# A one-layer decode kernel: five trips of the loop over head groups instead of four, and w_down split 11 rows per partition plus 128 rows on partitions 0 to 31

## The chip, the cores and the metric

The kernel runs on one core of a Trainium2 chip. The metric is device time of the whole program in microseconds (us); the kernel before has a median of 292.48 us over three runs (292.47 to 292.49). Engines are named as in the profile: PE is the matrix engine TensorE (PEld its weight loads), DVE VectorE, ACT ScalarE, POOL GpSimd, SP the engine that issues nearly all DMA transfers. A DMA transfer is cut into packets that up to 16 DMA engines move side by side.

## What is computed

One decode step of a transformer layer for two sequences, in bfloat16, with D = 640, 32 heads of 192, a window of the last 2048 cached positions, and a gated FFN of width F = 1536:

```python
x = A_x                                             # 2 x 1 x 640
q = layernorm(x) @ wq                               # 32 heads of 192
k, v = k_cache[..., -2048:, :], v_cache[..., -2048:, :]
h = x + softmax(q k^T / sqrt(192)) v @ wo
out = h + (gelu(layernorm(h) @ w_gate) * (layernorm(h) @ w_up)) @ w_down
```

Each weight and each cached key and value is used once, so the work is mostly reading: 122.29 MB come from HBM.

## The kernel before, in words

The program is written out as a list of operations with the tokens that each reads and writes (`_Prog`, from L50). From these it works out which semaphore each operation waits for. The operations of PE and DVE inside the loop get their wait values as a straight line in the trip number, so that one copy of the code serves all trips. This asks that every semaphore grows by the same amount in each trip; operations that do not run in every trip are counted on semaphores of their own (the class, `cls`, of an operation; the segments listed in `RARE`).

**The stream of loads.** SP issues all large loads in one order through one queue into a ring of 6 slots of 24,576 bytes per partition (`RING`, `pump`, L363). A load is issued as soon as what lay in its place has been used, so an SP instruction that waits holds back all loads behind it. The order is k(0), wq, k(1), then for g = 0 to 15 k(g+1) and v(g), with the output weights wo(0) behind v(3), wo(1) behind v(7), wo(2) and wo(3) behind v(15), and then w_gate, w_up and w_down. Each k or v tile is 3 MiB: one batch row, four heads, 2048 positions, with 64 positions of one head in the 24,576 bytes of each partition. w_down (1536 rows of 640) lies with 6 consecutive rows on each partition, twice, and comes in four transfers of 6, 3, 2 and 1 rows for each partition (`WDC`).

**The attention.** There are 16 tiles g, four to a group J of eight heads. For each g, PE turns the keys round (48 transposes at L574, copied out of PSUM by DVE at L588 and by ACT at L584), multiplies with the masked queries (`scores`, L635), DVE and ACT make the softmax (`softmax`, L644 to L655), PE brings the exponentials into columns (`e_columns`, L664), and `pv` (L680) adds up the values. `e_columns` and `pv` of tile g-1 are done between the steps of tile g. At the end of a group, `z_rows` (L694), `o_rows` (L705) and `o_columns` (L713) normalize and turn round the result, and `oproj(J)` (L731) multiplies with wo(J), one group later.

Tile 0, q and their masks stand ahead of the loop. The loop has four trips of tiles 4J+1 to 4J+4; in its fourth trip the last quarter is skipped. Behind the loop stand the end of tile 15, `o_rows(3)`, `oproj(2)`, `o_columns(3)` and `oproj(3)`.

**The end.** After `oproj(3)` comes the second layernorm, then for w_gate and w_up four matmuls for each of the five 128-row pieces c of D (`ffn_in`, L822; four column strips of 384 at once). `ffn_columns` (L831) turns the two results into columns with three transposes each; DVE and ACT make the gelu and the product `uT` (12 columns for each sequence). The w_down multiplication (L871) has 48 matmuls, four at a time, one transfer after the other; DVE copies the result (L877) and SP stores it (L878).

## Time and profile before

| what | value |
|---|---|
| median of the runs | 292.48 us (292.47 to 292.49) |
| the profiled execution's own time | 292.58 us |
| its span, first to last instruction | 291.3 us |
| around the span | 1.28 us |
| PE, DVE, ACT, POOL busy | 198.6, 122.8, 76.9, 25.7 us |
| mean granted clock of PE | 0.871 |
| bytes moved | 122.44 MB in 6506 packets, 420 GB/s over the span |

The profile is of one execution, which took 0.10 us longer than the median. Busy shares are of the span; the lines of the profile numbered L are those of the kernel before. A transfer lands when the last of its DMA engines has reported; the trace keeps one landing event for each engine that took part, and the start and length of each packet, but not which engine moved it.

### The profile page before, as it was taken

Reading aid. Unit: us, or ns where it says so; the run is one execution under the profiler, and the core shown is the slowest. Engines: PE = TensorE matmul, PEld = TensorE weight load, DVE = VectorE, ACT = ScalarE, POOL = GpSimd, SP = SyncE. Lnnn points to the kernel's source line nnn. Section 1 sums busy time; section 2 is a strip of 40 time slices with the busy share of each in tenths; the row PEclk is TensorE's granted clock in tenths of the full one; section 3 lists DMA queues with packets and bytes.
Section 4 is the critical chain, followed back from the end, with each engine's and each line's share of the span. In section 5 each row is a group of like instructions: output and inputs, shape, how many; then the busy total and the mean of one; then the engine's idle time right before and its main releaser. Section 6 shows DMA issues by size and latency. Waiting matters only on the chain.

```text
span 291.3 us, 5093 instructions
## 1 busy us (share of the span) xinstructions
PE 198.6 (68%) x2141; PEld 147.6 (51%) x2141; DVE 122.8 (42%) x231; ACT 76.9 (26%) x72; POOL 25.7 (9%) x85
## 2 busy tenths in 40 slices
PE   0650868786668288768677478868478778496684
PEld 0640437566355175637374475645465746472341
DVE  4350025455435334635356244635247445253331
ACT  1050014333322122423222123523142333151001
POOL 8820073000000000000000000000000000000000
PEclk9997568999979869997989579999689799688957
DMA  8999999999999999999999999999999999999994
GB/s 324 432 440 422 428 432 432 428 429 429 428 419 440 432 432 432 429 432 432 432 416 448 432 432 430 432 412 429 432 432 425 422 432 432 429 432 434 420 411 181
DMA packets 6506, 122.44 MB, mean 420 GB/s; under 512 B 734, under 2 KB 864, under 8 KB 1504
## 3 DMA queue, kind: packets, MB, share of 16 engines
q1 hardware_dynamic: 6348, 121.90, 97.8%
q10 hardware_dynamic: 148, 0.40, 0.4%
q8 instruction: 7, 0.11, 0.2%
q14 instruction: 3, 0.02, 0.0%
HBM read 122.29 MB, written 0.00 MB: 420 GB/s over the span
## 4 chain that ended last, share of the span: by engine, by line
DMA 73%; PE 18%; DVE 3%; issue 2%; SPq 2%; ACT 1%; DVEq 0%
DMA ring<-in_A_k_cache_dram 54%; PE tpp L574 13%; DMA ring<-in_A_wq_dram 10%; DMA ring<-in_B_w_down_dram 9%; DVE ktr L588 3%; PE tpp L598 2%; SPq L363 2%; PE ops L680 1%; DVE ering L428 1%; ACT ktr L584 1%; PE m L731 1%; PE m L713 1%; PE m L871 0%; PE m L694 0%; DVE yrow L877 0%
## 5 line engine op out<-in xcount | busy, mean ns | idle before, releaser
L574 PE MATMUL tpp<-identf,ring 128*128 128x128 f32 x768 | 116.2, 314 | 39.3 <-DMA ring<-in_A_k_cache_dram 25.2
L574 PEld LDWEIGHTS tpp<-identf,ring 128*128 128x128 f32 x768 | 102.8, 163 | 47.5 <-DMA ring<-in_A_k_cache_dram 26.5
L588 DVE COPY ktr<-tpp 128x2048 bf16<-128x2048 bf16 x64 | 78.4, 1224 | 91.4 <-PE tpp L574 91.4
L584 ACT ACTIVATE ktr<-tpp 128x2048 bf16<-128x2048 bf16 x32 | 60.1, 1877 | 94.9 <-PE tpp L574 94.9
L655 ACT ACTIVATE eexp<-sm,nm 128x512 bf16<-128x512 f32 x16 | 11.6, 722 | 71.7 <-DVE nm L653 71.7
L635 PE MATMUL sps<-ktr,rq 128*16 128x512 bf16 x384 | 25.7, 402 | 1.1 <-POOL rq L428 1.1
L680 PE MATMUL ops<-ring,ering 128*32 128x384 bf16 x512 | 25.0, 339 | 0.0
L644 DVE CUSTOM_DVE_ANT_1 sm<-sps,mska 128x512 f32<-128x512 f32 x16 | 11.0, 686 | 27.0 <-issue 27.0
L428 POOL TENSOR_TENSOR rq<-qs,mask 128x96 bf16<-128x96 bf16 x16 | 5.5, 354 | 175.6 <-PE sps L635 154.1
L680 PEld LDWEIGHTS ops<-ring,ering 128*32 128x32 bf16 x512 | 12.7, 99 | 8.5 <-issue 2.8
L635 PEld LDWEIGHTS sps<-ktr,rq 128*16 128x16 bf16 x384 | 8.9, 89 | 14.4 <-issue 5.5
L651 PEld LDWEIGHTS m<-mrhs,pm 128*128 128x128 bf16 x16 | 1.5, 96 | 22.9 <-DVE mrhs L424 22.9
L651 PE MATMUL m<-mrhs,pm 128*128 128x16 bf16 x16 | 2.9, 184 | 14.8 <-DVE mrhs L424 14.8
L598 PE MATMUL tpp<-ring,xnT 128*32 128x384 bf16 x80 | 6.1, 499 | 9.4 <-DMA ring<-in_A_wq_dram 9.4
L598 PEld LDWEIGHTS tpp<-ring,xnT 128*32 128x32 bf16 x80 | 3.4, 143 | 11.9 <-issue 9.6
L621 DVE CAST qs<-ops 128x384 bf16<-128x384 f32 x1 | 0.6, 558 | 15.8 <-PE ops L616 15.8
L428 DVE TENSOR_TENSOR ering<-m,mask 128x256 bf16<-128x256 f32 x16 | 6.6, 415 | 1.3 <-PE m L664 1.3
L713 PE MATMUL m<-selb,orow 128*128 128x2 bf16 x48 | 3.5, 200 | 5.2 <-DVE ering L428 4.5
L713 PEld LDWEIGHTS m<-selb,orow 128*128 128x128 bf16 x48 | 3.2, 159 | 6.0 <-DVE ering L428 4.9
L664 PE MATMUL m<-sel,eexp 128*128 128x64 bf16 x64 | 4.8, 200 | 1.2 <-ACT eexp L655 1.2
L494 PE MATMUL m<-identb,xrow 2*128 2x2 bf16 x5 | 0.3, 173 | 7.4 <-DMA xrow<-in_A_x_dram 7.4
L428 DVE TENSOR_TENSOR orow<-m,wm 128x1536 bf16<-128x1536 f32 x3 | 5.3, 1751 | 0.0
(127 smaller groups left out, 93.6 us busy)
## 6 DMA issues: line engine op xcount, KB each, us to landing
ring<-in_A_k_cache_dram SPq DMA_DIRECT2D x16, 3072.0 KB, 29.5
ring<-in_A_v_cache_dram SPq DMA_DIRECT2D x16, 3072.0 KB, 25.4
ring<-in_A_wq_dram SPq DMA_DIRECT2D x1, 7680.0 KB, 28.1
ring<-in_A_wo_dram SPq DMA_DIRECT2D x4, 1920.0 KB, 21.6
ring<-in_B_w_gate_dram SPq DMA_DIRECT2D x1, 1536.0 KB, 31.4
ring<-in_B_w_up_dram SPq DMA_DIRECT2D x1, 1536.0 KB, 21.9
ring<-in_B_w_down_dram SPq DMA_DIRECT2D x1, 960.0 KB, 24.3
ring<-in_B_w_down_dram SPq DMA_DIRECT2D x1, 480.0 KB, 25.0
```

Source lines behind the costliest of these rows:

```text
L363: P.op("sp", lambda e, v=v, src=src: e.dma_start(v, src), W=toks + [("sem", sem)], dma=sem)
L428: return lambda e: e.tensor_tensor(out=out, in0=a, in1=b, op=op)
L574: ins = e.transpose(tpp[bi][:, 512 * j + 128 * u:512 * j + 128 * (u + 1)], kv[:, off:off + 128], identf[:, :])
L584: act(lambda e, dst=dst, bv=bv: e.activation(out=dst, in_=bv, func=ACT.Copy), W=[("kt", half, k)], X=both)
L588: dve(lambda e, dst=dst, bv=bv: e.tensor_copy(dst, bv.rearrange("p (a x) -> p a x", a=2)), W=[("kt", half, k)], X=both, cls=0)
L598: ins = e.matmul(tps[0][32 * r:32 * (r + 1), 0:384], lhsT=xnT[:, c, 32 * J:32 * (J + 1)], rhs=wq[:, c, 1536 * J + 384 * r:1536 * J + 384 * ...
L635: ins = e.matmul(sps[32 * ch:32 * ch + 16, :], lhsT=rq[:, g % 4, k, :], rhs=ktr[:, k // 2, 1024 * ch + k % 2:1024 * (ch + 1):2], start=(k ...
L644: dve(lambda e: e.tensor_tensor_reduce(out=sm[:, :].rearrange("p (u x) -> p u x", u=4), in0=sps[:, :].rearrange("p (u x) -> p u x", u=4), ...
L655: act(lambda e: e.activation(out=eexp[:, :], in_=sm[:, :], func=ACT.Exp, bias=nm[:, 0:1], scale=1.0, accum_out=zr[:, g % 4:g % 4 + 1]), R= ...
L664: ins = e.matmul(o, lhsT=eexp[:, 128 * u:128 * (u + 1)], rhs=sel64[:, :], start=True, stop=True)
L680: ins = e.matmul(ops_[32 * r:32 * (r + 1), 0:384], lhsT=ering[:, g % 4, t, :], rhs=vv[:, 384 * t:384 * (t + 1)], start=(g % 4 == 0 and t < 4),
L713: ins = e.matmul(m2[:, 2 * kk:2 * kk + 2], lhsT=orow[:, :, kk:DH:12], rhs=selb[:, :], start=True, stop=True)
```

## The change

**The loop.** There are now five trips, and nothing of the attention but `oproj(3)` is left outside. A trip J begins with the transposes of tile 4J (not in the fifth). Then come, in trip 0 alone, `q_rows` and `q_stationary`; in the later trips the end of tile 4J-1 (`e_columns`, `z_rows`, `pv`, `o_rows`), from the third trip on `oproj(J-2)`, and `o_columns(J-1)`. Then, but for the fifth trip, scores and softmax of tile 4J, and the tiles 4J+1 to 4J+3. To keep the straight line of the waits, some semaphores start from an offset (`BIAS`, `WO_BIAS`), and there are three more of them. The program of PE has 744 matmuls in place of 858.

**Loads.** wo(0) is loaded behind v(7) in place of v(3), wo(1) behind v(11) in place of v(7), wo(2) behind v(15) as before, now into the slot of k(15). `oproj(2)` adds into `hrow` like the first two, and the residual x is added by two small matmuls in `oproj(3)` instead. w_up goes to the slot of k(14).

**w_down.** Rows 0 to 1407 lie with 11 consecutive rows on each partition, in transfers of 5, 3, 2 and 1 rows. The last 128 rows lie on partitions 0 to 31 alone, four rows each, in a transfer of their own (`wds`) ahead of the other four. Strip 3 of the gate and up results then is made of two matmuls, of 256 and 128 columns, so `ffn_in` has 5 matmuls for each c; `ffn_columns` has 9 transposes in place of 3; `uT` has 16 columns for each sequence, and w_down takes 60 matmuls in place of 48.

```diff
-WDC = ((0, 6), (6, 9), (9, 11), (11, 12))
+WDC = ((0, 5), (5, 8), (8, 10), (10, 11))
+NS = 11
-WO_AT = (K_AT[3], K_AT[3], K_AT[2], 0)
+WO_AT = (K_AT[3], K_AT[3], K_AT[3], 0)
+WU_AT = K_AT[2]
+WDS_AT = K_AT[1] + 12288
...
-            wd = B_w_down.rearrange("(q p s) n -> q p s n", p=128, s=6)
+            load("wds", WDS_AT, 8 * D, B_w_down[128 * NS:F, :].rearrange("(c a u) n -> a c (u n)", a=8, u=4), lambda v: v[0:32, :], "wds")
+            wd = B_w_down[0:128 * NS, :].rearrange("(p s) n -> p s n", s=NS)
...
-            if g % 4 == 3 and g < NG - 5:
-                load_wo(g // 4)
-        load_wo(2)
+            if g % 4 == 3 and g > 3:
+                load_wo(g // 4 - 1)
         load_wo(3)
...
-                    if J == 2:
+                    if J == 3:
                         for h in range(2):
                             e.matmul(m1[32 * h:32 * h + 2, 192:512], lhsT=identb[0:2, 0:2], rhs=xrow[0:2, 320 * h:320 * (h + 1)],
...
+        looped.append(True)
+        for J in range(5):
+            if J < 4:
+                P.loop_seg("d0", J)
+                transposes(4 * J, 0)
+                transposes(4 * J, 1)
+            if J == 0:
+                P.loop_seg("q", J)
+                q_rows()
+                q_stationary()
+            else:
+                P.loop_seg("y0", J)
+                e_columns(4 * J - 1)
+                z_rows(J - 1)
+                pv(4 * J - 1)
+                o_rows(J - 1)
+            if J > 1:
+                P.loop_seg("op", J)
+                oproj(J - 2)
+            if J > 0:
+                P.loop_seg("oc", J)
+                o_columns(J - 1)
+            if J < 4:
+                P.loop_seg("a0", J)
+                scores(4 * J)
+                softmax(4 * J)
+                for g in range(4 * J + 1, 4 * J + 4):
+                    transposes(g, 0)
+                    e_columns(g - 1)
+                    transposes(g, 1)
+                    pv(g - 1)
+                    scores(g)
+                    softmax(g)
         P.loop_seg()
-        e_columns(15)
...
-        oproj(2)
-        o_columns(3)
         oproj(3)
...
-                        for r in range(4):
-                            cols = wv[:, c - l0, 768 * (r // 2):768 * (r // 2 + 1)].rearrange("p (x s) -> p x s", s=6)
-                            ins = e.matmul(bank[32 * r:32 * r + 2, 0:384], lhsT=hnT[:, c, :], rhs=cols[:, :, 3 * (r % 2):3 * (r % 2) + 3],
-                                           start=(c == 0), stop=(c == NC5 - 1), tile_position=(0, 32 * r))
+                        cols = wv[:, c - l0, 0:128 * NS].rearrange("p (x s) -> p x s", s=NS)
+                        for r in range(3):
+                            e.matmul(bank[32 * r:32 * r + 2, 0:384], lhsT=hnT[:, c, :], rhs=cols[:, :, 3 * r:3 * r + 3],
+                                     start=(c == 0), stop=(c == NC5 - 1), tile_position=(0, 32 * r))
+                        e.matmul(bank[96:98, 0:256], lhsT=hnT[:, c, :], rhs=cols[:, :, 9:11], start=(c == 0), stop=(c == NC5 - 1),
+                                 tile_position=(0, 96), skip_group_check=True)
+                        ins = e.matmul(bank[96:98, 256:384], lhsT=hnT[:, c, :], start=False,
+                                       rhs=wv[:, c - l0, 128 * NS:F].rearrange("p (c a u) -> p a c u", c=4, a=8),
+                                       stop=(c == NC5 - 1), tile_position=(0, 96), skip_group_check=True)
...
-                    ins = e.transpose(bank[:, 128 * j:128 * j + 98], row[0:98, j:384:3], identf[0:98, 0:98])
+                    e.transpose(bank[:, 128 * j:128 * j + 66], row[0:66, j:384:3], identf[0:66, 0:66])
+                for j in range(2):
+                    e.transpose(bank[:, 128 * j + 96:128 * j + 98], row[96:98, j:256:2], identf[96:98, 96:98])
+                for u in range(4):
+                    ins = e.transpose(bank[0:32, 384 + 32 * u:386 + 32 * u], row[96:98, 256 + u:384:4], identf[96:98, 96:98])
...
+        def wds_rows(e):
+            for u in range(4):
+                for r in range(4):
+                    ins = e.matmul(m1[32 * r:32 * r + 17, 0:160], lhsT=uT[0:32, 12 + u, 0:17], rhs=wds[:, D * u + 160 * r:D * u + 160 * (r + 1)],
+                                   start=False, stop=False, tile_position=(0, 32 * r), skip_group_check=True)
+            return ins
...
-        order = ["a0", (0, None, ["oc"]), "a1", (0, 3, ["op"]), "a2", "b0", "b1", "b2", "c0", "c1", "c2", (None, 3, ["d0", "d1", "d2"])]
-        P.emit_loop("dve", nc.vector, sems, 4, order)
-        P.emit_loop("pe", nc.tensor, sems, 4, order)
+        order = [(None, 4, ["d0", (None, 1, ["q"])]), (0, None, ["y0", (1, None, ["op"]), "oc"]), (None, 4, ["a0"])]
+        P.emit_loop("dve", nc.vector, sems, 5, order)
+        P.emit_loop("pe", nc.tensor, sems, 5, order)
```

More of the change, by code (lines that the diff above doesn't have):

```diff
@@ L28 @@
 LOOPED = ("pe", "dve")
-RARE = ("oc", "op")
+BIAS = 16
+WO_BIAS = 32
+RARE = ("oc", "q", "y0")
 class _Op:
@@ L73, in op @@
     def op(self, eng, fn, R=(), W=(), X=(), dma=None, cls=0):
-        if eng == "pe" and self.seg in RARE:
+        if self.seg == "op" and eng in LOOPED:
+            cls = 2
+        elif eng == "pe" and self.seg in RARE:
             cls = 1
@@ L159, in resolve @@
         for e, l in self.per.items():
-            n = {}
+            n = {c: BIAS for c in (1, 2) if e in LOOPED}
             for o in l:
@@ L193, in emit_one @@
         elif o.need_inc:
-            ins.then_inc(sems[o.key()], 1)
+            ins.then_inc(sems[o.key()], 1 + BIAS if o.cls in (1, 2) and o.idx == 1 and o.eng in LOOPED else 1)
     def emit(self, name, eng, sems, ops=None):
@@ L330, in bass_sequential_preLN__sliding_block_cached__geglu_ffn__decode_kernel @@
         urow = osb
-        gsb = sb("gsb", [128, NF * B], F32)
-        ga = sb("ga", [128, 4, NF * B], F32)
-        uT = sb("uT", [128, NF, 18], BF16)
+        gsb = sb("gsb", [128, 16 * B], F32)
+        ga = sb("ga", [128, 4, 16 * B], F32)
+        uT = sb("uT", [128, 16, 18], BF16)
         tpp = [ps(f"tpp{i}", [128, 1024], F32) for i in range(2)]
@@ L342, in bass_sequential_preLN__sliding_block_cached__geglu_ffn__decode_kernel @@
         P = _Prog()
+        P.dma_count["wo"] = WO_BIAS
+        looped = []
         where, live, queue, used = {}, [], [], set()
@@ L386, in load_wo @@
                 load(("wo", J, i), WO_AT[J] + 2 * k0 * D, 2 * (k1 - k0) * D, src[:, k0:k1, :],
-                     lambda v: v.rearrange("p (kk n) -> p kk n", n=D), "wo" if J < 2 else f"wo{J}{i}")
+                     lambda v: v.rearrange("p (kk n) -> p kk n", n=D), "wo" if J < 3 else f"wo{J}{i}")
         def wo_parts(J):
@@ L399, in load_ffn, with act @@
             for i, (c0, c1) in enumerate(WUC):
-                load(("wu", i), K_AT[3] + 2 * c0 * F, 2 * (c1 - c0) * F, B_w_up.rearrange("(p c) f -> p c f", c=NC5)[:, c0:c1, :],
+                load(("wu", i), WU_AT + 2 * c0 * F, 2 * (c1 - c0) * F, B_w_up.rearrange("(p c) f -> p c f", c=NC5)[:, c0:c1, :],
                      lambda v: v.rearrange("p (c f) -> p c f", f=F), f"wu{i}")
-            wd = B_w_down.rearrange("(q p s) n -> q p s n", p=128, s=6)
+            load("wds", WDS_AT, 8 * D, B_w_down[128 * NS:F, :].rearrange("(c a u) n -> a c (u n)", a=8, u=4), lambda v: v[0:32, :], "wds")
+            wd = B_w_down[0:128 * NS, :].rearrange("(p s) n -> p s n", s=NS)
             for i, (f0, f1) in enumerate(WDC):
-                q = f0 // 6
-                load(("wd", i), WD_AT[i], 2 * (f1 - f0) * D, wd[q][:, f0 - 6 * q:f1 - 6 * q, :],
+                load(("wd", i), WD_AT[i], 2 * (f1 - f0) * D, wd[:, f0:f1, :],
                      lambda v: v.rearrange("p (s n) -> p s n", n=D), f"wd{i}")
         def dve(fn, R=(), W=(), X=(), cls=1):
-            return P.op("dve", fn, R, W, X, cls=cls)
-        def act(fn, R=(), W=(), X=()):
-            return P.op("act", fn, R, W, X)
+            return P.op("dve", fn, R, W, X, cls=cls if looped else 0)
+        def act(fn, R=(), W=(), X=(), cls=0):
+            return P.op("act", fn, R, W, X, cls=cls)
         def pe(fn, R=(), W=(), X=(), cls=0):
@@ L454, in bass_sequential_preLN__sliding_block_cached__geglu_ffn__decode_kernel @@
         pool(lambda e: e.memset(uT[:, :, :].rearrange("p a b -> p (a b)").bitcast(I32), 0), W=["uT"])
-        dve(lambda e: e.memset(eps_t[:, :], EPS), W=["eps"])
-        dve(lambda e: e.memset(onesd[:, :], 1.0 / D), W=["onesd"])
+        P.op("dve", lambda e: e.memset(eps_t[:, :], EPS), W=["eps"], cls=1)
+        P.op("dve", lambda e: e.memset(onesd[:, :], 1.0 / D), W=["onesd"], cls=2)
         dve(lambda e: e.memset(xnT[:, :, :].rearrange("p a b -> p (a b)").bitcast(I32), 0), W=["xnT"])
@@ L475, in layernorm @@
             pe(lambda e: e.matmul(m2[:, 16:18], lhsT=onesd[:, :], rhs=ls[:, 0, :], start=True, stop=True),
-               R=["onesd", "ls0"], X=["m2"])
+               R=["onesd", "ls0"], X=["m2"], cls=2)
             dve(lambda e: e.tensor_copy(mean[:, :], m2[:, 16:18]), W=["mean"], X=["m2"])
@@ L496, in _x_T @@
             return ins
-        pe(_x_T, R=["xrow", "identb"], X=["m2"])
+        pe(_x_T, R=["xrow", "identb"], X=["m2"], cls=1)
         dve(lambda e: e.tensor_copy(xT[:, :, :].rearrange("p c b -> p (c b)"), m2[:, 0:10]), W=["xT"], X=["m2"])
@@ L607, in q_rows @@
                 in_=tps[0][:, 0:384].rearrange("p (h d) -> p h d", h=2).unsqueeze(2).to_broadcast([128, 2, 2, DH]),
-                func=ACT.Copy, scale=SCALE), W=["qrow"], X=[("t", 0)])
+                func=ACT.Copy, scale=SCALE), W=["qrow"], X=[("t", 0)], cls=1)
         def q_stationary():
@@ L671, in e_columns @@
                    mask16[:, :].rearrange("p (h x) -> p h x", h=2).unsqueeze(1).to_broadcast([128, 16, 2, 8]), ALU.mult),
-                R=["mask16"], W=[("er", g % 4)], X=["m2"], cls=0)
+                R=["mask16"], W=[("er", g % 4)], X=["m2"], cls=int(g % 4 == 3))
         def pv(g):
@@ L701, in o_rows @@
         def o_rows(J):
-            bank, tok = (m1, "m1") if J < 3 else (sps, "s")
+            bank = m2[:, 276:276 + DH]
             for tp in range(2):
-                pe(lambda e, tp=tp: e.matmul(bank[:, 0:DH], lhsT=selw[:, tp, :], rhs=osb[:, DH * tp:DH * (tp + 1)], start=(tp == 0),
-                                             stop=(tp == 1), skip_group_check=True), R=[("osb", tp), ("selw", tp)], X=[tok])
-            dve(tt(orow[:, :, :], bank[:, 0:DH].unsqueeze(1).to_broadcast([128, 8, DH]),
-                   wm[:, :].unsqueeze(2).to_broadcast([128, 8, DH]), ALU.mult), R=["wm"], W=["orow"], X=[tok])
+                pe(lambda e, tp=tp: e.matmul(bank, lhsT=selw[:, tp, :], rhs=osb[:, DH * tp:DH * (tp + 1)], start=(tp == 0),
+                                             stop=(tp == 1), skip_group_check=True), R=[("osb", tp), ("selw", tp)], X=["m2o"])
+            dve(tt(orow[:, :, :], bank.unsqueeze(1).to_broadcast([128, 8, DH]),
+                   wm[:, :].unsqueeze(2).to_broadcast([128, 8, DH]), ALU.mult), R=["wm"], W=["orow"], X=["m2o"])
         def o_columns(J):
@@ L731, in fn @@
                             ins = e.matmul(m1[32 * r:32 * r + 2, 192:512], lhsT=ot[:, kk, :],
-                                           rhs=wo[:, kk - k0, 320 * h:320 * (h + 1)], start=(kk == 1 or J < 2 and kk == 0) and J < 3,
-                                           stop=(J != 2 and kk >= 10), tile_position=(0, 32 * r), skip_group_check=True)
+                                           rhs=wo[:, kk - k0, 320 * h:320 * (h + 1)], start=(kk == 1 or J < 3 and kk == 0),
+                                           stop=(kk >= 10), tile_position=(0, 32 * r), skip_group_check=True)
                     return ins
@@ L737, in oproj @@
                 done(("wo", J, i))
-            if J < 2:
+            if J < 3:
                 dve(tt(hrow[0:98, :], m1[0:98, 192:512], hrow[0:98, :], ALU.add), R=["hrow"], W=["hrow"], X=["m1"])
@@ L752, in h_columns @@
             pe(fn, R=["hrow", ("hsel", 0), ("hsel", 1)], X=["m2"])
-        transposes(0, 0)
-        transposes(0, 1)
-        q_rows()
-        q_stationary()
         consts_late()
-        scores(0)
-        softmax(0)
-        for J in range(4):
-            for p in range(1, 5 if J < 3 else 4):
-                g = 4 * J + p
-                seg = "abcd"[p - 1]
-                P.loop_seg(seg + "0", J)
-                transposes(g, 0)
-                e_columns(g - 1)
-                if p == 4:
-                    z_rows(J)
-                if p == 1 and J > 0:
-                    P.loop_seg("oc", J)
-                    o_columns(J - 1)
-                P.loop_seg(seg + "1", J)
-                transposes(g, 1)
-                if p == 1 and 0 < J < 3:
-                    P.loop_seg("op", J)
-                    oproj(J - 1)
-                P.loop_seg(seg + "2", J)
-                pv(g - 1)
-                scores(g)
-                if p == 4:
-                    o_rows(J)
-                softmax(g)
-        P.loop_seg()
-        e_columns(15)
-        z_rows(3)
-        pv(15)
-        o_rows(3)
-        oproj(2)
-        o_columns(3)
+        looped.append(True)
[31 more added lines that the diff above has]
+                    softmax(g)
+        P.loop_seg()
         oproj(3)
@@ L830, in fn @@
                 for j in range(3):
-                    ins = e.transpose(bank[:, 128 * j:128 * j + 98], row[0:98, j:384:3], identf[0:98, 0:98])
+                    e.transpose(bank[:, 128 * j:128 * j + 66], row[0:66, j:384:3], identf[0:66, 0:66])
[3 more added lines that the diff above has]
+                    ins = e.transpose(bank[0:32, 384 + 32 * u:386 + 32 * u], row[96:98, 256 + u:384:4], identf[96:98, 96:98])
                 return ins
             pe(fn, R=[*tok, "identf"], X=[("t", i)])
-            return bank[:, 0:384].rearrange("p (j r y) -> p r j y", j=3, y=32)[:, :, :, 0:2]
+            return bank[:, :].rearrange("p (k y) -> p k y", y=32)[:, :, 0:2]
         def h_rows(e):
@@ L841, in h_rows, with kb @@
             return ins
-        def rjb(t):
-            return t.rearrange("p (r j b) -> p r j b", r=4, j=3)
+        def kb(t):
+            return t.rearrange("p (k b) -> p k b", b=B)
         ffn_in(sps, "s", "wg", ((0, 1), (1, 2)), ((0, 1), (1, NC5)))
@@ L850, in bass_sequential_preLN__sliding_block_cached__geglu_ffn__decode_kernel @@
         pe(h_rows, R=["hrow", ("hsel", 0), ("hsel", 1)], X=["m1"])
-        gT = ffn_columns(grow, ["sm"], tps[0], 0)
-        dve(lambda e: e.tensor_copy(rjb(gsb[:, :]), gT), W=["gsb"], X=[("t", 0)])
+        gT = ffn_columns(grow[:, 0:384], ["sm"], tps[0], 0)
+        dve(lambda e: e.tensor_copy(kb(gsb[:, :]), gT), W=["gsb"], X=[("t", 0)])
         dve(tt(ga[:, 0, :], gsb[:, :], gsb[:, :], ALU.mult), R=["gsb"], W=["ga0"])
@@ L863, in bass_sequential_preLN__sliding_block_cached__geglu_ffn__decode_kernel @@
         vT = ffn_columns(urow, [("osb", 0), ("osb", 1)], tps[1], 1)
-        dve(tt(uT[:, :, 0:17:16].rearrange("p (r j) b -> p r j b", r=4), vT, rjb(ga[:, 0, :]), ALU.mult), R=["ga0"], W=["uT"], X=[("t", 1)])
+        dve(tt(uT[:, :, 0:17:16], vT, kb(ga[:, 0, :]), ALU.mult), R=["ga0"], W=["uT"], X=[("t", 1)])
+        wds, wtoks = where["wds"]
+        def wds_rows(e):
[4 more added lines that the diff above has]
+            return ins
+        pe(wds_rows, R=["uT"] + wtoks, X=["m1"])
         for i, (f0, f1) in enumerate(WDC):
@@ L870, in fn @@
                     for r in range(4):
-                        ins = e.matmul(m1[32 * r:32 * r + 17, 0:160], lhsT=uT[:, f, 0:17],
-                                       rhs=wd[:, f - f0, 160 * r:160 * (r + 1)], start=False, stop=(f == NF - 1),
+                        ins = e.matmul(m1[32 * r:32 * r + 17, 0:160], lhsT=uT[:, 4 * (f % 3) + f // 3, 0:17],
+                                       rhs=wd[:, f - f0, 160 * r:160 * (r + 1)], start=False, stop=(f == NS - 1),
                                        tile_position=(0, 32 * r), skip_group_check=True)
@@ L879, in bass_sequential_preLN__sliding_block_cached__geglu_ffn__decode_kernel @@
              dma="dout")
-        P.resolve({("dve", 0): 4 * 9, ("dve", 1): 8, ("act", 0): 4 * 3, ("pool", 0): 4})
+        P.resolve({("dve", 0): 4 * 9 - 1, ("dve", 1): 8, ("dve", 2): 1, ("act", 1): 0, ("act", 0): 4 * 3, ("pool", 0): 4})
         sems = {}
-        for e, c in (("pe", 0), ("pe", 1), ("act", 0), ("dve", 0), ("dve", 1), ("pool", 0)):
+        for e, c in (("pe", 0), ("pe", 1), ("pe", 2), ("dve", 2), ("act", 0), ("act", 1), ("dve", 0), ("dve", 1), ("pool", 0)):
             sems[e, c] = ctx.enter_context(nc.semaphore(f"s_{e}{c}"))
@@ L889, in bass_sequential_preLN__sliding_block_cached__geglu_ffn__decode_kernel @@
         nc.sync.wait_ge(sems["d", "dout"], 16)
+        nc.gpsimd.sem_inc(sems["d", "wo"], WO_BIAS)
         P.emit("pool", nc.gpsimd, sems)
         P.emit("act", nc.scalar, sems)
-        order = ["a0", (0, None, ["oc"]), "a1", (0, 3, ["op"]), "a2", "b0", "b1", "b2", "c0", "c1", "c2", (None, 3, ["d0", "d1", "d2"])]
-        P.emit_loop("dve", nc.vector, sems, 4, order)
-        P.emit_loop("pe", nc.tensor, sems, 4, order)
+        order = [(None, 4, ["d0", (None, 1, ["q"])]), (0, None, ["y0", (1, None, ["op"]), "oc"]), (None, 4, ["a0"])]
+        P.emit_loop("dve", nc.vector, sems, 5, order)
+        P.emit_loop("pe", nc.tensor, sems, 5, order)
 _INS = ['A_x', 'A_k_cache', 'A_v_cache', 'A_wq', 'A_wo', 'B_x', 'B_w_gate', 'B_w_up', 'B_w_down']
```

## The prediction

> **What bounds the kernel now.** I read the page first: the slices, the queues, the chain. Then the end of the span in order of time, and the trace's landing events.

> ```profile
> PEclk9997568999979869997989579999689799688957
> DMA  8999999999999999999999999999999999999994
> GB/s 324 432 440 422 428 432 432 428 429 429 428 419 440 432 432 432 429 432 432 432 416 448 432 432 430 432 412 429 432 432 425 422 432 432 429 432 434 420 411 181
> ...
> q8 instruction: 7, 0.11, 0.2%
> ...
> DMA 73%; PE 18%; DVE 3%; issue 2%; SPq 2%; ACT 1%; DVEq 0%
> ```

> From the second slice to the last but one the DMA engines are 90% busy or more, at about 430 GB/s. The loads are never starved, and the chain is theirs for 73%. So nothing inside the loop counts as long as loads are issued in time. What counts is when the last byte lands, and what follows.

> ```profile
> 275.86 0.99 PE L731 MATMUL m<-ring,ot 128*2 128x320 bf16 x24 [1.16 <-DMA ring<-in_A_wo_dram]
> ...
> 282.44 0.77 PE L831 MATMUL tpp<-identf,sm 98*128 98x98 f32 x3 [0.20 <-DVE sm L424]
> ...
> 283.13 1.67 PE L822 MATMUL ops<-ring,hnT 128*2 128x384 bf16 x20
> ...
> 285.49 0.59 PE L831 MATMUL tpp<-identf,osb 98*128 98x98 f32 x3 [0.69 <-ACT osb L861]
> ...
> 286.51 0.59 PE L871 MATMUL m<-ring,uT 128*17 128x160 bf16 x24 [0.44 <-DMA ring<-in_B_w_down_dram]
> 287.59 0.39 PE L871 MATMUL m<-ring,uT 128*17 128x160 bf16 x12 [0.49 <-DMA ring<-in_B_w_down_dram]
> 288.39 0.72 PE L871 MATMUL m<-ring,uT 128*17 128x160 bf16 x12 [0.42 <-DMA ring<-in_B_w_down_dram]
> ```

> PE waits for each w_down transfer. The last lands at 288.76; its four matmuls start at 288.80; then come DVE (289.17), the store, and the end at 291.3. That tail stays.

> The landing events say more. The sixteen of the last transfer come from 286.89 to 288.76: a spread of 1.87 us. The first large transfers spread over 0.4 to 0.6 us. Each of the instruction fetches in queue q8 (16,384 bytes, about 1.0 us; at 33, 54, 64, 76, 93, 275 and 287 us) makes one DMA engine about 1.5 us late, and it stays late. By following packets from end to start I get sixteen rows of packets: the five engines hit first are five different ones, 1.7 to 1.9 us late at the end; the one hit at 275 is 1.5 late; the fetch at 287 finds an engine already done. **The last load therefore lands when the five late engines are through; the others idle for up to 1.87 us.**

> **The loads, part by part.**

> *w_down.* If the 128 rows go through eight DMA engines, these get 4 packets of 5120 bytes more. All sixteen get 6400 in place of 7680 bytes in each of eight packets. Packets of 7680 and 3840 bytes took 295 and 149 ns, 25.9 bytes per ns: so 8 x 1280 / 25.9 = 0.39 us less on each engine, and 4 x 5120 / 25.9 = 0.79 more on eight, net +0.40 on these and -0.39 on the others. The best case is that all five late ones are relieved: **-0.39 us** on the last landing, to 288.37.

> Does it go through eight? The two-row x reported from two engines; the store, 4 x 2 pieces, landed with twelve events at once and four later, so it used four. The new transfer's outer sizes are 8 in memory and 32 in SBUF; I take eight. [...]

> Are the late ones the other eight? The trace numbers no engine. But the five were among the six that landed the first k tile last (0.24 to 0.40 us after the first), and the one hit at 275 among the early (under 0.1). The two rows of packets that hold x, a transfer on fewer engines, had started third and sixth of sixteen. If such transfers use the early starters, the five are relieved. I take that at 7 in 10.

> *The shorter PE program.* Before: 858 matmuls, 24 of them f32 products in two passes, so 882 pairs of weight load and matmul, and 61 other instructions: 1825. Between the fetches at 275 and 287 PE shows 255 records, and 1825 / 255 is 7.2: seven fetches. After: 744 + 21 pairs and 69 others, 1599, 6.3: six. Stepping back 255 at a time from the seventh (48 before the end), the fifth then falls 48 instructions behind the loop, in `oproj(3)` at about 276 us, and the sixth 77 before the end, in the w_down matmuls, too late to matter. So the early-landing engine's hit at 275 goes, and the fifth comes late but still costs its 1.5. The worst lateness stays: 0 us from this part alone. But that engine would have become the last (1.5 + 0.40).

> *Moved loads.* SP takes the wo loads past four k and four v tiles; the bytes are the same. Before, SP issued wo(2), wo(3) and w_gate at 246.9 to 248.4. Now wo(2) needs the slot of k(15), free at 261.18, and all loads behind it wait too. v(15) lands from 264.57 on; an issue reaches its packets within 2.35 us (k(0): 0.72 to 3.07; the store: 1.3), so at 263.5 at the latest: a margin of 1 us, price 0. k(11) and k(15) now wait for `oproj(0)` and `oproj(1)`, with 3 to 4 tiles (7.3 us each) still under way: 0.

> *Engine programs.* The branches, the 16 further waits on ACT, and POOL's 14 masks (6.7 us, 39.3 to 46.0) moved ahead of the query masks, where POOL had idled 21.5 us, lie under the loads: PE waits 25 us in all for k tiles, and had waited 2.9 us for k(15). Nothing, unless PE falls about 2 us behind at k(15).

> **The path of PE behind wo(3),** which has little slack, gets longer. wo(3) lands at 275.7 as before.

> ```profile
> 279.00:281.00 2.00, 1.73 (x22) 0.78 (x24) 0.64 (x4) 0.28 (x2) 0.00 (x0) 0.50 0.93 390
> 281.00:283.00 2.00, 1.80 (x23) 0.74 (x11) 0.62 (x1) 0.18 (x1) 0.00 (x0) 0.50 1.02 417
> 283.00:285.00 2.00, 1.80 (x22) 0.44 (x20) 1.30 (x7) 0.37 (x2) 0.00 (x0) 0.64 1.01 412
> 285.00:287.00 2.00, 1.08 (x27) 0.84 (x27) 0.32 (x2) 0.43 (x1) 0.00 (x0) 1.00 0.88 344
> 287.00:289.00 2.00, 1.09 (x32) 0.40 (x24) 0.00 (x0) 0.00 (x0) 0.00 (x0) 0.71 0.27 98
> ```

> The figure after POOL is PE's granted clock: half until 284.4, full until 287.8, then half again.

> - x moved into `oproj(3)`: its two matmuls ran 271.89 to 272.12: +0.23 (0.14, one step of L731, to 0.29, their busy time).
> - Five matmuls per c: the same columns, now one behind the other in strip 3. L822 steps by 0.32 per c at half clock, so 128 columns are 0.11: between 0 and 3 x 0.11 for gate, 0 and 5 x 0.11 for up. I take 0.10 each, nearer to no more columns.
> - Six more transposes, of two rows each. Nearest: a pass of L748 (64 columns, 20 in 1.07: 0.053) and a step of L831 (0.16 at half, 0.12 at full clock). Gate 0.32 to 0.97, up 0.32 to 0.71. Two have 128 columns, four 32: I take 0.45 and 0.40. Ahead of up there is a slack of 0.23: weight loads ended at 282.90, w_up landed at 283.06, matmuls at 283.13.
> - 16 more w_down matmuls: 15 groups of four. A group took 0.068 at full clock and 0.096 at half (288.395 to 288.491): 14 steps are 0.95 to 1.35; I take 1.20, as the clock may fall halfway.

> Sum: 286.51 + (0.23 + 0.10 + 0.45 - 0.23) + 0.10 + 0.40 = 287.56 for the first group, and the last starts at 288.76. The loads would allow 288.41, and before it was 288.80. So PE ends the span now. With the 1.20 the change is -0.04 us, with full clock (0.95) -0.29; I take **-0.15** between them: 292.58 - 0.15 = 292.43 for the profiled execution, which stood 0.10 above the median; so **292.3**.

> **The rivals.**
> 1. *PE's end takes over in earnest* (slower). All upper ends: 286.51 + (0.29 + 0.33 + 0.97 - 0.23) + 0.55 + 0.71 = 289.13, and 1.35 more: 290.48, 1.68 later than 288.80, 294.2. It decides from a sum 0.04 us above mine, and reaches slower by over 0.2% (about what a measurement of this kernel can tell from no change, 0.58 us) at 0.62 above. For it: half clock and chained small steps; against: two-row transposes are little work. Above 0.2%: 0.20, typically 293.4; below: 0.10, 292.7.
> 2. *Late engines are among the eight loaded:* last landing +0.40, 292.9. For: no numbers in the trace. 0.15.
> 3. *The rows spread over sixteen engines,* or the change does nothing at the end: 292.5. 0.06.
> 4. *Branches make PE fetch again:* five trips over some 1200 instructions, 4 to 5 fetches a trip, so engines are hit twice: +1.5, 294.0. Against: no q8 packet between 92.7 and 275.1, over three trips of 1000. 0.03. [...]
> 5. *Faster:* the late engines recover more than the eight packets give, say half their lateness, 0.9: 291.6. Nothing shows it. 0.06.

> **How the numbers follow.** Forecast 0.40 (292.1 to 292.6). Faster by over 0.2%: 0.06; slower: rivals 1 (upper) and 4, 0.23; within: 0.71. The range, 292.0 to 293.4, leaves out the fifth, the fourth and half of the first: 0.19.

> **What would show it.** Six q8 packets, the fifth near 276; the last transfer's landings closer together (about 1.5 us); the last w_down group starting less than 0.1 us after a wait on DMA if loads still bound it, or without a wait if PE does; first w_down matmul near 287.6. A DMA slice under 9 near 263, q8 packets in every trip, or late engines beyond 2.2 us would prove me wrong.

## The result, and the profile after

| | median, us | runs | ratio of the runs to the kernel before, 95% interval |
|---|---|---|---|
| kernel before, measured beside it | 292.72 (292.43 to 292.84) | 15 | |
| kernel after | 294.24 (292.66 to 294.55) | 15 | 1.0045 (1.0036 to 1.0053) |

It is slower by 0.45%, where the prediction had 292.3 and no change that can be measured. The time of the kernel after is not one number: one of its fifteen runs took 292.66, six took 293.25 to 293.64 and eight 294.24 to 294.55, while those of the kernel before fill 0.4 us. The profiled execution is one of the better ones: 293.33 us, span 292.0.

Its page has the loads as before, as busy as before, but a chain that has gone over to the engines:

```profile
PEclk9996699997979779999799998999799969797558
DMA  8999999999999999999999999999999999999993
...
q8 instruction: 6, 0.10, 0.1%
...
DMA 58%; PE 22%; DVE 8%; issue 8%; ACT 3%; SPq 1%; DVEq 0%
```

DMA falls from 73% of the chain to 58%; PE, DVE, issue and ACT rise. There are six instruction fetches, as forecast. The end of the span in order of time tells the rest (start, duration, engine, line, operation, and in brackets what ended the wait before it):

```profile
275.78 0.42 PE L732 MATMUL m<-xrow,identb 2*2 2x320 bf16 x2 [0.79 <-DMA ring<-in_A_wo_dram]
276.13 1.77 PE L737 MATMUL m<-ring,ot 128*2 128x320 bf16 x24
277.95 0.49 DVE L747 CUSTOM_DVE_ANT_0 hrow<-m,hrow 98x320 f32<-98x320 f32 x1 [2.75 <-PE m L737]
...
284.29 0.31 PEld L842 LDWEIGHTS tpp<-identf,sm 2*128 2x128 f32 x2
284.51 0.23 PEld L844 LDWEIGHTS tpp<-identf,sm 2*32 2x32 f32 x4
284.75 0.09 PEld L826 LDWEIGHTS ops<-ring,hnT 128*2 128x2 bf16 x3
...
288.57 0.45 PE L883 MATMUL m<-ring,uT 32*17 32x160 bf16 x16 [0.34 <-DVE uT L436]
288.95 0.94 PE L894 MATMUL m<-ring,uT 128*17 128x160 bf16 x44
289.94 0.33 DVE L900 CAST yrow<-m 113x160 bf16<-113x160 f32 x1 [1.43 <-PE m L894]
```

The line to read first is L894: 44 w_down matmuls in one piece, with no bracket. Before, the w_down matmuls stood in four groups, each behind a wait for its transfer. Now the last transfer has landed at 288.84, the 16 matmuls of `wds` (L883) have started at 288.57, and L894 starts at 288.95 without a wait: PE ends the span. Read upwards for where the time was lost: wo(3) lands at 275.7 as before, but the sum `hrow` starts at 277.95, w_up at 284.75 (before 283.13), and the first w_down matmul 2.06 us later than before. The line of `hrow` before:

```profile
276.90 0.49 DVE L741 CUSTOM_DVE_ANT_0 hrow<-m,hrow 98x320 f32<-98x320 f32 x1 [1.98 <-PE m L731]
```

The windows view has the granted clock of PE, as a share of full speed, in the third figure from the end (0.50 is called half clock here):

```profile
277.00:279.00 2.00, 1.39 (x18) 0.65 (x10) 0.50 (x2) 0.00 (x0) 0.00 (x0) 0.50 1.05 442
281.00:283.00 2.00, 2.00 (x31) 1.21 (x26) 0.08 (x1) 0.46 (x2) 0.00 (x0) 0.50 0.99 401
285.00:287.00 2.00, 1.54 (x25) 0.69 (x17) 1.34 (x7) 0.65 (x2) 0.00 (x0) 1.00 0.89 350
289.00:291.00 2.00, 0.89 (x48) 0.68 (x44) 0.33 (x1) 0.00 (x0) 0.00 (x0) 0.77 0.00 0
```

Here the clock was half from 266.2 to 283.25 and full from there to 290.1. In the execution of before it was full at `oproj(3)`, where the 24 matmuls took 0.99 in place of 1.77 us.

### The profile page after: what moved, and what is told of

Same layout as the page of the kernel before. It is cut to its first block, busy times and chain, and to the rows that moved or that the text cites. A ratio compares the mean times of both kernels' runs of the same rounds, so it can differ in the third digit from the quotient of the medians.

```text
span 292.0 us, 5262 instructions
## 1 busy us (share of the span) xinstructions
PE 198.5 (68%) x2175; PEld 145.2 (50%) x2175; DVE 123.9 (42%) x232; ACT 76.9 (26%) x72; POOL 25.9 (9%) x85
## 4 chain that ended last, share of the span: by engine, by line
DMA 58%; PE 22%; DVE 8%; issue 8%; ACT 3%; SPq 1%; DVEq 0%
DMA ring<-in_A_k_cache_dram 43%; PE tpp L581 12%; DMA ring<-in_A_wq_dram 10%; DVE ktr L595 5%; DMA ring<-in_A_wo_dram 5%; ACT ktr L591 3%; PE ops L687 2%; PE tpp L605 2%; PE m L737 1%; DVE ering L436 1%; SPq L371 1%; PE m L711 1%; DVE orow L436 1%; PE sps L826 1%; PE m L754 0%
## 5 line engine op out<-in xcount | busy, mean ns | idle before, releaser
L581 PE MATMUL tpp<-identf,ring 128*128 128x128 f32 x768 | 112.4, 306 | 39.4 <-DMA ring<-in_A_k_cache_dram 21.8
L581 PEld LDWEIGHTS tpp<-identf,ring 128*128 128x128 f32 x768 | 97.9, 158 | 49.9 <-DMA ring<-in_A_k_cache_dram 22.9
L605 PE MATMUL tpp<-ring,xnT 128*32 128x384 bf16 x80 | 5.4, 452 | 9.3 <-DMA ring<-in_A_wq_dram 9.3
L436 DVE TENSOR_TENSOR orow<-m,wm 128x1536 bf16<-128x1536 f32 x4 | 7.0, 1758 | 4.1 <-PE m L711 4.1
L711 PE MATMUL m<-osb,selw 128*128 128x192 f32 x16 | 4.4, 406 | 1.9 <-DVE osb L697 1.9
L737 PE MATMUL m<-ring,ot 128*2 128x320 bf16 x96 | 5.5, 381 | 0.0
```

Of the source, the lines that this page charges most:

```text
L436: return lambda e: e.tensor_tensor(out=out, in0=a, in1=b, op=op)
L581: ins = e.transpose(tpp[bi][:, 512 * j + 128 * u:512 * j + 128 * (u + 1)], kv[:, off:off + 128], identf[:, :])
L605: ins = e.matmul(tps[0][32 * r:32 * (r + 1), 0:384], lhsT=xnT[:, c, 32 * J:32 * (J + 1)], rhs=wq[:, c, 1536 * J + 384 * r:1536 * J + 384 * ...
L711: pe(lambda e, tp=tp: e.matmul(bank, lhsT=selw[:, tp, :], rhs=osb[:, DH * tp:DH * (tp + 1)], start=(tp == 0), stop=(tp == 1), skip_group_c ...
L737: ins = e.matmul(m1[32 * r:32 * r + 2, 192:512], lhsT=ot[:, kk, :], rhs=wo[:, kk - k0, 320 * h:320 * (h + 1)], start=(kk == 1 or J < 3 and ...
```

## The experiments

**Theories.** (1) PE's path behind wo(3) ends the span, lengthened by the work of the new w_down layout. (2) The last landing is later, because late DMA engines are among the eight that carry the 128 rows. (3) The five-trip loop itself costs. (4), formed after the first four runs: the new work would hide, but for the granted clock of PE, which is half over much of the tail, the part behind the loop. Medians are beside 292.71 to 292.82 us of the kernel before in the same series; intervals are of the ratio to it.

**The loop alone**: w_down, `ffn_in` and `ffn_columns` put back.

```diff
-WDC = ((0, 5), (5, 8), (8, 10), (10, 11))
-NS = 11
+WDC = ((0, 6), (6, 9), (9, 11), (11, 12))
...
```

> The five-trip loop alone; w_down as before (6 rows twice, four transfers, four matmuls per c, three transposes per row set, twelve groups). Theory 1 (TensorE's path behind wo(3) ends the span, and the new w_down layout is what lengthened it): the path loses 4 groups of about 0.067 us, the further transposes and the fifth matmul per c, some 1 us in all, so that the loads end the span again: the w_down matmuls wait for a DMA before the last transfer, the last group starts at 288.8 to 289.0, 292.5 to 292.8. Theory 2 (the last landing moved because the eight loaded DMA engines include late ones): the last landing goes back from 288.84 to 288.76 or less, and as that is only 0.08, the time hardly follows: 294.1. Theory 3 (the loop itself costs: later instruction fetches, x in the last projection, the clock): as the changed kernel, 294.0 to 294.4.

Measured: 292.80 us (292.40 to 293.19), 1.0002 (0.9993 to 1.0010). The last w_down group waits for a DMA again and starts at 288.93. The loop, the moved loads and x in `oproj(3)` cost nothing that shows, so theory 3 falls in its plain form. Yet in this profile the clock was half from 274.9 to 285.1, the 24 matmuls of `oproj(3)` took 1.77 us, and the first w_down matmul came at 287.48, 0.97 later than before: most of the slack was used up.

**The split alone**, on the four-trip loop (the new layout put into the kernel before).

> The four-trip loop and order of the kernel before, with the new w_down layout alone. Theory 1: all of the further TensorE work of the layout and none of the x matmuls: first w_down matmul at 287.4 to 288.3 by the clock, then sixty matmuls in 0.95 to 1.35 without a wait on DMA; 292.6 to 293.9, with a wider spread between runs than before (0.4 us). Theory 2: set by which DMA engines are late: 292.1 if the eight loaded ones are the early ones, 292.9 if not, and a w_down group that waits on DMA. Theory 3 (the loop itself): 292.5, as before.

Measured: 293.06 us (292.79 to 293.93), 1.0013 (1.0005 to 1.0022). The profiled run, 293.58, is the second slowest of the eleven. It was at half clock from 278.35 to the end, with its w_down matmuls from 287.86 to 290.14 and no wait for a DMA: theory 1, here at its small end. Whether PE also ended the span in the median run isn't shown. Together, loop and split cost 1.5 us; singly 0.0 and 0.3. That is what one slack looks like when two changes draw on it.

The profiles suggest what the loop takes from it. In the two profiles of four-trip kernels the half clock begins at 277.6 and 278.35, and the 24 matmuls of `oproj(3)` take 0.99 us. In the eight of five-trip kernels without the fill of the later runs it has begun by 276.65, ahead of `oproj(3)` or within it, and they take 1.12 to 1.77. Two profiles on one side are too few to call it shown.

**The rows over sixteen engines**, with the columns of gate and up to match.

```diff
-            load("wds", WDS_AT, 8 * D, B_w_down[128 * NS:F, :].rearrange("(c a u) n -> a c (u n)", a=8, u=4), lambda v: v[0:32, :], "wds")
+            load("wds", WDS_AT, 8 * D, B_w_down[128 * NS:F, :].rearrange("(a c u) n -> a c (u n)", a=16, u=4), lambda v: v[0:32, :], "wds")
...
-                                       rhs=wv[:, c - l0, 128 * NS:F].rearrange("p (c a u) -> p a c u", c=4, a=8),
+                                       rhs=wv[:, c - l0, 128 * NS:F].rearrange("p (a c u) -> p a c u", c=2, a=16),
```

> The changed kernel with the 128 w_down rows spread over sixteen DMA engines (an outer size of 16 in place of 8); TensorE's work is the same. Theory 1: the last landing changes by up to 0.4 us and nothing waits for it; 294.0 to 294.4, within 0.2% of the changed kernel. Theory 2 (landing ends the span): the three relieved engines lose 0.39 and the two loaded late ones gain it, last landing 288.45, 293.85.

Measured: 294.50 us (293.82 to 294.63), 1.0062 (1.0049 to 1.0075). It doesn't answer the question it was for: the last landing was not 288.45 but 290.00, and the last group started behind it, at 290.04. Packets of every size had taken 1.2 to 1.6 times as long between 282.0 and 285.5. So it was run again:

> The rows over sixteen DMA engines once more. In the first profile every packet between 282.0 and 285.5 us took 1.2 to 1.6 times as long, whatever its size, and the last landing was 290.0. If that belongs to the spread over sixteen engines it comes again at the same place; if it was an accident of that execution, the last landing is 288.7 to 288.9 and TensorE ends the span at half clock: 294.2 to 294.6 either way in the median.

Measured: 294.13 us (293.82 to 294.73), 1.0054 (1.0040 to 1.0069), with the slow stretch at the same place and the last landing at 290.07. The last two figures of a windows line are the DMA share and GB/s:

```profile
280.00:282.00 2.00, 2.00 (x26) 1.18 (x30) 0.40 (x2) 0.46 (x2) 0.00 (x0) 0.50 0.96 390
282.00:284.00 2.00, 1.82 (x22) 1.05 (x15) 0.62 (x1) 0.00 (x0) 0.00 (x0) 0.63 1.02 259
284.00:286.00 2.00, 1.88 (x30) 0.91 (x28) 1.33 (x7) 0.31 (x2) 0.00 (x0) 1.00 1.00 306
286.00:288.00 2.00, 1.11 (x17) 0.96 (x21) 0.40 (x2) 0.50 (x1) 0.00 (x0) 1.00 0.99 383
```

The engines stay fully busy, but from 282 to 286 they move 259 and 306 GB/s, where the kernel after moves 418 and 396. It came in two profiles of two, and in none of the eleven others: it belongs to this spread of the rows, and the last landing is about 1.2 us later for it. Why, these runs don't say. For the split on eight engines they tell nothing.

**x ahead of the loop.**

```diff
-                    if J == 3:
-                        for h in range(2):
-                            e.matmul(m1[32 * h:32 * h + 2, 192:512], lhsT=identb[0:2, 0:2], rhs=xrow[0:2, 320 * h:320 * (h + 1)],
...
+        pe(x_rows, R=["xrow", "identb"], X=["m1"], cls=1)
+        dve(lambda e: e.tensor_copy(hrow[0:34, :], m1[0:34, 192:512]), R=["hrow"], W=["hrow"], X=["m1"])
```

> The changed kernel with the two x matmuls taken out of the last projection: x is put into the sum of the projections ahead of the loop. Theory 1: the path behind wo(3) loses the 0.35 us that the two took in the profile at half clock (0.14 at full): 293.8 to 294.1, still bound by TensorE. Theory 2: 294.24, no change. Theory 3, in the form that x is all of the loop's cost: 292.5 to 293.

Measured: 293.56 us (292.94 to 294.36), 1.0034 (1.0022 to 1.0046). The median is 0.7 below the kernel after, twice the 0.35 of the two matmuls at half clock, and meets none of the three expectations. That it gains more than those 0.35 isn't shown: the intervals overlap (1.0036 to 1.0053 for the kernel after), and profile against profile, both at full clock from about 283, the gain is 0.39 (293.33 to 292.94). But it raised the question whether a step taken off a path also changes the clock behind it. That led to theory 4.

**Fill.** The changed kernel, with matmuls whose result nobody reads where PE waits in the tail.

```diff
+        def fill(n, w, bank):
+            def fn(e):
+                for _ in range(n):
+                    ins = e.matmul(bank[:, 512 - w:512], lhsT=identb[:, :], start=True, stop=True, skip_group_check=True,
+                                   rhs=identb[:, 0:w // 4].unsqueeze(1).to_broadcast([128, 4, w // 4]))
...
+        fill(3, 480, tps[3])
         oproj(3)
+        fill(2, 480, tps[3])
```

> The changed kernel with fill: matmuls of 480 (or 240) columns of a constant into an unused PSUM bank, put where TensorE waits in the last 30 us (three ahead of the last trip, four ahead of its last columns, three ahead of oproj(3), then two, one, one and two behind it), 3.3 us in all at full clock. Theory 4 (the granted clock: full clock drops after a 3.41 us window with little TensorE work, and the half clock of the tail is what makes the new work late): the clock stays full from 267 us to the end in most of the tail, the first w_down matmul comes before 287.6, the loads end the span again, 292.6 to 293.0, with a spread of runs under 0.8. Theory 1 in the form that it is the work itself: the fill can't help, 294.0 to 294.8, as every fill that outlasts its wait adds to the path.

Measured: 293.16 us (292.27 to 293.79), 1.0006 (0.9996 to 1.0015): over a microsecond is given back by adding work. But the profile doesn't have what theory 4 asked for: the clock still was half from 276.4 to 283.3, the first w_down matmul came at 288.39 and not before 287.6, PE still ended the span, and the runs spread over 1.5 us, not under 0.8. With more fill (seven ahead of `oproj(3)`, and more at most of the other places):

> The changed kernel with more fill: four, four and seven ahead of oproj(3), then three, one, two and four behind it, 5 us at full clock. Theory 4 (the granted clock): the half-clock stretch gets shorter or goes, the first w_down matmul comes before 287.6, the loads end the span, 292.8 to 293.2 (the last landing is 289.1 in three of the changed kernel's profiles). Against it: 293.2 as with less fill, or over 293.5 where the fill outlasts its waits.

Measured: **292.71 us** (292.39 to 293.17), 1.0001 (0.9992 to 1.0010), against 292.71 of the kernel before.

```profile
277.00:279.00 2.00, 2.00 (x26) 1.61 (x24) 0.48 (x3) 0.00 (x0) 0.00 (x0) 1.00 1.02 430
281.00:283.00 2.00, 2.00 (x29) 1.14 (x16) 0.62 (x1) 0.00 (x0) 0.00 (x0) 1.00 1.00 406
285.00:287.00 2.00, 1.66 (x21) 1.18 (x23) 0.35 (x2) 0.47 (x1) 0.00 (x0) 1.00 0.91 353
```

In this profile the clock is full from 243.0 to 290.8, and in the order of time the waits for transfers are back:

```profile
286.87 0.45 PE L903 MATMUL m<-ring,uT 32*17 32x160 bf16 x16 [0.34 <-DVE uT L436]
...
288.62 0.64 PE L914 MATMUL m<-ring,uT 128*17 128x160 bf16 x12 [0.40 <-DMA ring<-in_B_w_down_dram]
...
289.31 0.33 DVE L920 CAST yrow<-m 113x160 bf16<-113x160 f32 x1 [2.50 <-PE m L914]
```

All the work of the change is in this kernel, and it hides. The first w_down matmul comes 1.52 us earlier than with less fill, in a kernel that differs only in having more matmuls at the same places. That is theory 4 shown: work alone does not make the change slow, work at half clock does. It rests on one profile and eleven runs. In eight of these the mean granted clock was 0.902 to 0.910, in place of 0.921 to 0.924 in the profiled one and two more, and they were no slower; where in the span it fell in them isn't known.

**Loop, x early and fill together**, without the split.

> The five-trip loop without the new w_down layout, with x put in ahead of the loop and the fill: the lightest tail that I can build from the parts. If TensorE's path is what delays: nothing but the last landing ends the span, every run near the low end of the loop alone, 292.3 to 292.6. If something else in the five-trip loop costs: 292.8 as the loop alone. A gain of over 0.2% on the kernel before isn't expected, as the last landing stays at 288.8.

Measured: 292.80 us (292.39 to 292.92), 0.9997 (0.9989 to 1.0006). The first w_down matmul was at 286.46 and the last group at 288.72, behind its transfer. The lightest tail I have is no faster than the kernel before: the loads end it. No version beat the kernel before.

**Loads only**: the new loads, with PE's tail work cut back to that of before. It leaves out part of the gate, up and w_down products.

> The changed kernel with its loads (128 rows through eight DMA engines) but with TensorE's tail work cut to that of the kernel before: four matmuls of 384 columns per c, three transposes, twelve groups of w_down matmuls. It leaves out part of the product, so its output is not the reference's. Theory 1: the new loads cost nothing by themselves, the work does: 292.6 to 293.0. Theory 2 (the loads): the last landing depends on which engines are late, 288.5 to 289.2, and 293.2 or more in the median.

Measured: 293.06 us (292.47 to 293.42), 1.0009 (1.0000 to 1.0018).

```profile
287.65 0.73 PE L887 MATMUL m<-ring,uT 128*17 128x160 bf16 x32
288.57 0.64 PE L887 MATMUL m<-ring,uT 128*17 128x160 bf16 x12 [0.20 <-DMA ring<-in_B_w_down_dram]
288.97 0.10 PEld L887 LDWEIGHTS m<-ring,uT 128*17 128x17 bf16 x4 [0.28 <-DMA ring<-in_B_w_down_dram]
```

Half clock to 285.3 here, and the loads still end it: the cut path fits. The median is 0.26 above the loop alone, in another series; as ratios it is 1.0009 against 1.0002 with overlapping intervals, so these runs alone don't show that the new loads cost anything.

**Work only**: the old loads, with PE's further work. The further transposes and w_down matmuls write where nobody reads; the fifth matmul per c takes over a part of the fourth one's columns.

> The five-trip loop with the loads of the kernel before and only TensorE's further work of the new layout, as matmuls whose results nobody reads: a fifth matmul per c, six small transposes more in each row set, twelve w_down matmuls more ahead of the sixty-minus-twelve real ones. Theory 1 (the work on TensorE's path, stretched by the clock): as the changed kernel less the 0.26 that its loads cost by the runs before, 294.0 to 294.5, a last w_down group that waits for no DMA, half clock over the w_down matmuls in most runs. Theory 2 (the loads do it, or loads and work only together): 292.8 to 293.1.

Measured: 294.38 us (293.52 to 294.70), 1.0049 (1.0036 to 1.0061).

```profile
289.37 1.78 PE L889 MATMUL m<-ring,uT 128*17 128x160 bf16 x48
291.20 0.33 DVE L895 CAST yrow<-m 113x160 bf16<-113x160 f32 x1 [2.39 <-PE m L889]
```

No wait for a DMA, half clock from 275.6 to the end. On five trips this makes a square: old loads and old work 292.80, new loads 293.06, new work 294.38, both 294.24 to 294.52. Theory 2 has at most 0.26, theory 1 the rest, at the clock of theory 4, and where PE ends the span the later landing is hidden.

**The kernel after once more.**

> The changed kernel once more on the chip of these runs, for a second profile: 294.0 to 294.4 in the median, 292.7 to 294.6 over the runs, the half clock beginning elsewhere in the tail, as the 3.41 us windows run freely.

Measured: 294.52 us (292.78 to 294.81), 1.0041 (1.0026 to 1.0056), a little above what was expected. The profiled run took 294.54:

```profile
288.81 0.71 PE L883 MATMUL m<-ring,uT 32*17 32x160 bf16 x16 [0.34 <-DVE uT L436]
289.45 1.65 PE L894 MATMUL m<-ring,uT 128*17 128x160 bf16 x44
291.15 0.32 DVE L900 CAST yrow<-m 113x160 bf16<-113x160 f32 x1 [2.40 <-PE m L894]
```

It reaches w_down only 0.24 us later than the first profile of this kernel, but takes 2.34 in place of 1.37 us from there to the copy by DVE (L894 alone 1.65 in place of 0.94): the clock, half from 276.1, never came back. These two differences are the 1.21 us between the two profiled runs. Over the 26 runs of this kernel, the seven with a mean granted clock of 0.891 or more took 292.66 to 293.64 us, the nine below 0.880 took 294.24 to 294.81.

## Why the prediction was wrong, point by point

**The step that failed** is the sum of PE's path behind wo(3), "286.51 + (0.23 + 0.10 + 0.45 - 0.23) + 0.10 + 0.40 = 287.56 for the first group, and the last starts at 288.76". In the two profiles of the kernel after, the first group started at 288.57 and 288.81, and the last at 289.65 and 290.75. The work added ahead of w_down was sized nearly right. But the times that it was added to were those of one execution, and its clock was taken for the kernel's; and the w_down matmuls at half clock were sized too small.

- *x in `oproj(3)`, +0.23:* it took 0.35 and 0.22. But the 24 matmuls behind it went from 0.99 to 1.77 at half clock, +0.78, a term that the sum doesn't have. `hrow` was 1.05 and 1.03 later.
- *Five matmuls per c, +0.10 each:* for gate, from the first matmul to the scaling, 2.35 before and 2.52 after, both at half clock: +0.17. For up, from the first matmul to the scaling by ACT, 1.72 before and 1.83 at full clock, 2.00 at half.
- *Six more transposes, +0.45 and +0.40:* gate +0.50 (0.96 from the first transpose to w_up; before, the weight loads of the three ended 0.46 after their start, and w_up then waited for its transfer), up +0.43 (1.05 from the first to `uT` in place of 0.62; 1.11 at half clock). Right.
- *16 more w_down matmuls, 14 steps of 0.068 to 0.096, taken as 1.20:* at full clock 1.08 (first profile), but at half clock 1.94 (second), +0.74. The 0.096 was read from a single step, the first one behind a wait. That first step is 0.100 in the second profile too; nearly all that follow are 0.133. The row of L894 in the second profile, eleven groups in 1.65 us, fits that.
- *The second profile*, the nearer to the median, has its last group 1.99 later than the sum: 1.25 of it in the path, 0.78 of that in the 24 matmuls alone, and 0.74 in the w_down steps.
- *The rival that won* is the first, "PE's end takes over in earnest", at 0.20 and with its typical 293.4 a microsecond short of the median. Its direction was right. That its upper end, 294.2, meets the median is luck: it has the first group at 289.13, 0.32 later than the second profile, as the small transposes were priced up to 0.97, and then 1.35 for w_down, 0.59 less than measured. Nothing in it has the 24 matmuls at half clock. 14 of 26 runs took 294.24 or more.

**The w_down term, -0.39, failed too**, with less at stake. The transfer does go through eight engines, the author's assumption in the prediction: it has 32 packets of 5120 bytes and eight landing events (282.96 to 284.51) besides an early one (264.18), and the next transfer's landings fit eight engines with their lateness as it was and eight that are 0.80 later, to within 0.04 us. (The store, from which the prediction argued, shows one early landing event in the trace, at 290.59, and four later ones, at 291.17 to 291.23, not twelve and four; that four engines carried it follows all the same.) "The five are relieved" is what went wrong. Comparing the landings of w_up with those of the next transfers, two of the five latest engines are among the loaded eight in all six profiles of five-trip kernels with this split. From w_up's last landing to the last landing of all it is 4.69 to 4.73 us in four profiles without the split, and 4.75 to 5.10, mean 4.94, in those six: +0.23 in place of -0.39. In the four-trip kernel with the split none of its five is loaded, as the prediction had it, and it has 4.53; there a sixth engine, 1.69 late at w_up and loaded, ends it, as the prediction feared of the one hit at 275 (that it is that one isn't shown). So the mechanism fitted the old program's fetches, and the new program's seem to hit other engines. This is rival 2, 292.9 forecast, and 293.06 measured with the loads alone, which its interval barely tells from no change. In the kernel after it is hidden, as PE ends the span.

**The shorter PE program:** six fetches as forecast, five of them before the last landing. The fifth was not fixed at 276: it came at 266.1 and 276.0 in two profiles of the same kernel, at 204 in one of the two with sixteen engines, at 139 with the first fill and at 82 with x early. No profile has a fetch in every trip, so rival 4 falls; the first has none between 66 and 266 us.

**Moved loads and engine programs, 0:** right as far as the runs show. SP issued wo(2) to w_down from 260.7 to 265.8 with the DMA engines at 97% from 262 to 267, and the loop alone is at 1.0002.

Of the signs that were named, the first w_down matmul (287.6 against 288.57), the last group without a wait and the landings (2.16 apart, not 1.5) all spoke in the first profile. In the second they are 2.36 apart, beyond the 2.2 that was to prove the prediction wrong.

## What to carry to other kernels

A path that hides behind loads in one profile has a slack for one state of the clock: size all of it at half clock as well, the steps that the change doesn't touch included (the 24 matmuls of `oproj(3)` took 0.99 us at full clock and 1.77 at half), and give that case the chance that the windows of the trace show. Read the length of a step from several in a row, not from the first one behind a wait (0.100 us for the first step of the w_down matmuls in the second profile, 0.133 for nearly all that followed). Where sparse work follows a wait, matmuls that nobody reads can be worth more than the work that they sit beside (292.71 us with more fill, 294.24 and 294.52 without). And the shorter program of PE also moved its instruction fetches (seven before, from 33 to 287 us, and six after, from 34 to 288), so the late DMA engines of the old trace need not be those of the new one (two of the five latest were among the loaded eight in six profiles).

## What the runs showed of the hardware

**With the rows over sixteen DMA engines, packets were slower for a while.** The same 32 pieces of 5120 bytes went over sixteen engines in place of eight, and packets of every size took 1.2 to 1.9 times as long from 282.0 to 285.5 us, in both profiles (those of 6400 bytes 470 and 431 ns between 282 and 283, in place of 248). It isn't explained.

**Left open:** which DMA engines PE's fetches hit, and whether they are the same in each execution; the trace doesn't number them.
